# Weights before values: moving the second half of the up weights, its groups and the values' casts in a fused attention and feed-forward kernel

## The chip, the cores and the metric

The kernel runs on one core of a Trainium2 chip. The metric is the device time of one execution in microseconds (us). Six runs of the kernel before gave a median of 352.59 us (351.64 to 352.95).

The engines by their names in the profile: PE is TensorE (matmuls; PEld its weight loads), DVE is VectorE, ACT is ScalarE, POOL is GpSimd, SP is SyncE, which here only issues transfers. POOL computes and issues transfers, in one order.

## The reference

There are 8 sequences of 576 tokens, with 8 heads of 64 columns, and 16 beacon keys and values in front of each head's own. Attention is causal over the 576, and the beacons are seen by all. Its output, 4608 rows of 512 columns, goes through a two-layer feed-forward part with a leaky ReLU.

```
q, k, v: (8, 8, 576, 64); beacon_k, beacon_v: (8, 8, 16, 64)
k_all = concatenate([beacon_k, k], axis=2); v_all likewise
scores = q @ k_all^T / sqrt(64), causal over the 576, beacons always seen
a = softmax(scores);  attn = a @ v_all
x = attn as (4608, 512)
h = x @ w_in            # (512, 2048), the "up" weights
g = maximum(0.01 * h, h)
out = g @ w_out         # (2048, 512)
```

## The kernel before, in words

**Tiling.** Attention goes by head pairs. There are four pairs in a sequence, so g = 0 to 31; g = 0 to 3 is sequence 0, g = 4 to 7 is sequence 1. For each pair:

- `score(g, n)`, n = 0 to 3, makes a part of the transposed scores (L306) in one of two PSUM buffers, and ScalarE writes its exponential to `aT` (L315). There are four `aT` buffers.
- `masks(g)` zeroes the part above the diagonal, by four POOL instructions (L363).
- `value(g, half)` multiplies `aT` with the values and a column of ones (L394); VectorE takes the reciprocal of the sums (L403) and scales (L404) into `x_nat`. Half 0 has three row blocks and needs key blocks 0 to 2 of the values; half 1 has two and needs all five.
- `finish(g)` transposes `x_nat` on TensorE (L416), and VectorE copies it to `xT` (L421), the feed-forward input with d_model on the partitions. It also sets `ready`, the number of chunks of 512 tokens whose `xT` is whole: one after g = 3, two after g = 7.

The feed-forward part goes by these chunks (nine) and, in each, by groups of four matmuls. `moe1(i, fc)` computes 128 of the 2048 hidden columns of chunk i (L430, then ScalarE at L437); 16 groups make a chunk, and groups 0 to 7 need the first half of `w_in`, 8 to 15 the second. `moe2` does a quarter of one of four output blocks (L452); after four, VectorE copies the result (L461) and SP stores it. Quarters 0 and 1 use the first half of `w_out`, 2 and 3 the second.

**Order.** All five engines follow an order written out by hand: an instruction stands on its engine where the code has it. `fill()` puts one feed-forward group at its place: a first-layer group if `xT` is ready, a second-layer group if its chunk is through and enough first-layer groups are done, by turns when both can go. If neither can go it puts nothing.

**The values.** `load_v(b)` puts six fp32 transfers for a sequence on SP's queue (L213, L216, L218): the beacons, then the five key blocks (the first without its beacons). With `after` given, the first waits until another transfer has landed. `cast_v` turns key blocks to bf16 in `v_aug`, one instruction a block (L227), and needs the loads landed.

**Transfers on POOL's queue.** `load_w_in(half)` (L110) and `load_w_out(half)` (L114) load half of a weight matrix each, fp32 to bf16. `load_qk(b, grp, es)` loads q and k of two head pairs (grp 0 or 1) as bf16; `es` takes one of the two (L133). `load_beacon_k` (L175) loads the beacon keys of sequences 2 to 7.

**Transposing q and k.** In sequences 0 and 1, `t_q(g, which)` transposes on TensorE (L253) and copies on VectorE. From sequence 2 on, `permute` (POOL, L167) reorders, `turn_pairs` transposes by two transfers on SP (L271), and `in_order(g)` puts the result in order on POOL: the beacon columns (L284), then qT and kT (L286). The beacon columns come from `beacon_transposes` (TensorE L189, VectorE L194), which needs `cast_beacon_k`.

**Around the change.** The steps g = 5, 6, 7 and the beginning of g = 8 are written out one by one. Here sequence 1's scores, all of sequence 1's values and the 16 first-layer groups of chunk 0 share TensorE. From g = 8 on a loop spreads the groups evenly over eight slots a step.

Of the kernel before, what the change touches and what calls it, by code (L numbers as in the profile page):

```python
# [15 lines left out]
def kernel(  # L16
# [11 lines left out]
    nc = tc.nc  # L28
# [9 lines left out]
    NF = DF // 128  # L38
# [69 lines left out]
    def load_w_in(half):  # L108
        cols = slice(half * DF // 2, (half + 1) * DF // 2)
        return nc.gpsimd.dma_start(out=w_in_sb[:, :, cols], in_=w_in_r[:, :, cols])  # L110
# [98 lines left out]
    def load_v(b, after=None):  # L209

        t = rawpool.tile([128, NKB, H, D], FP32, name="v_raw")
        v_raws[b] = t
        first = nc.sync.dma_start(out=t[0:NB, 0], in_=beacon_v[b].rearrange("h p d -> p h d"))  # L213
        if after is not None:
            behind(first, after)
        nc.sync.dma_start(out=t[NB:128, 0], in_=v[b, :, 0:112].rearrange("h p d -> p h d"))  # L216
        for c in (1, 2, 3, 4):
            last = nc.sync.dma_start(  # L218
                out=t[0 : ROWS[c], c],
                in_=v[b, :, OFF[c] : OFF[c] + ROWS[c]].rearrange("h p d -> p h d"),  # L220
            )
        return last

    def cast_v(b, eng, c0=0, c1=NKB):
        t, dst = v_raws[b], v_bufs[b % 2]
        for c in range(c0, c1):
            eng.tensor_copy(out=dst[0 : ROWS[c], c, :, 0:D], in_=t[0 : ROWS[c], c])  # L227
# [240 lines left out]
    def fill():  # L468
        i1, fc = divmod(done1[0], NF)
        i2, n2 = divmod(done2[0], NF)  # L470
        can1 = i1 < ready[0] and (i1 < 2 or i2 > i1 - 2)
        can2 = i2 < NCH and i2 < i1 and done1[0] >= NF + 10
        if can1 and (turn[0] == 0 or not can2):
            moe1(i1, fc)
            done1[0] += 1
            turn[0] = 1
        elif can2:
            moe2(i2, n2 // 4, n2 % 4)
            done2[0] += 1
            turn[0] = 0  # L480
        return can1 or can2
# [24 lines left out]
    with order:  # L506
# [23 lines left out]
        def loads(g):  # L530
            b, hp = divmod(g, NPAIR)
            if g == 1:
                cast_v(0, nc.gpsimd, 0, 1)
                load_qk(1, 0, (0,))
                beacon_columns(3, nc.gpsimd)
                cast_v(0, nc.gpsimd, 1, 3)
                load_v(1, after=load_qk(1, 0, (1,)))
                load_w_in(0)
                cast_v(0, nc.gpsimd, 3, 5)
            elif g == 2:  # L540
                beacon_columns(4, nc.gpsimd)
            elif g == 3:
                load_qk(1, 1, (0,))
                beacon_columns(5, nc.gpsimd)
            elif g == 4:
                load_qk(1, 1, (1,))
                beacon_columns(6, nc.gpsimd)
            elif g == 5:
                beacon_columns(7, nc.gpsimd)
            elif g > 2 * NPAIR and b < B - 1 and hp > 1:  # L550
                turn_pairs(b + 1, hp - 2)
                if hp == 2:
                    load_v(b + 1)
# [27 lines left out]
        for g in range(NG + 3):  # L581
            if has(g):
                loads(g)

            if g < 5:

                score(g, 0)
                score(g, 1)
                t_q(g + 1, 0)
                t_q(g + 1, 1)  # L590
                if g == 1:
                    tri_in_psum()
                if g in (1, 2):
                    masks_by_tri(g - 1)
                if g == 4:
                    value(2, 0)
                if g < 2:
                    keep_busy(3)
                score(g, 2)
                if g < 2:  # L600
                    keep_busy(7)
                if g == 3:
                    value(0, 1)
                score(g, 3)
                if g < 2:
                    keep_busy(4)
                if g == 2:
                    value(0, 0)
                elif g == 3:
                    value(1, 0)  # L610
                    value(1, 1)
                    finish(0)
                elif g == 4:
                    value(2, 1)
                    finish(1)
                if g > 1:
                    masks(g)
                if g == 4:
                    value(3, 0)
                continue  # L620

            if g == 5:

                score(5, 0)
                value(3, 1)
                score(5, 1)
                finish(2)
                score(5, 2)
                finish(3)
                fill()  # L630
                score(5, 3)
                cast_v(1, nc.gpsimd, 0, 3)
                load_w_in(1)
                masks(5)
                fill()
                t_q(6, 0)
                t_q(6, 1)
                fill()
                fill()
                continue  # L640

            if g == 6:
                score(6, 0)
                score(6, 1)
                fill()
                t_q(7, 0)
                t_q(7, 1)
                fill()
                score(6, 2)
                score(6, 3)  # L650
                cast_v(1, nc.gpsimd, 3, 5)
                load_w_out(0)
                masks(6)
                load_w_out(1)
                load_beacon_k(2, B, nc.gpsimd)
                fill()
                fill()
                value(4, 0)
                value(4, 1)
                continue  # L660

            if g == 7:
                score(7, 0)
                score(7, 1)
                value(5, 0)
                finish(4)
                value(5, 1)
                score(7, 2)
                fill()
                score(7, 3)  # L670
                load_qk(2, 0)
                masks(7)
                value(6, 0)
                finish(5)
                fill()
                value(6, 1)
                fill()
                value(7, 0)
                finish(6)
                fill()  # L680
                value(7, 1)
                fill()
                fill()
                finish(7)
                continue

            if g == 8:
                load_qk(2, 1)
                cast_beacon_k(2, B, nc.gpsimd.tensor_copy)
                for grp in range(2):  # L690
                    for which in range(2):
                        permute(2, grp, which)
                    turn_pairs(2, grp)
                    if grp == 0:
                        load_v(2)
                while done1[0] + done2[0] < 22:
                    fill()
                beacon_transposes(2, B)
                while done1[0] + done2[0] < 32:
                    fill()  # L700
                in_order(8)
                in_order(9)


            chunks = chunks_with(g - 3) if g - 3 >= 2 * NPAIR else ready[0]
            groups = 2 * NF * chunks - done1[0] - done2[0]
            steps = NPAIR - (g - 2) % NPAIR if g > 2 * NPAIR + 5 else 2 * NPAIR + 6 - g
            n = -(-(groups - 1) // steps)
            slots = [0] * 8
            for i in range(n):  # L710
                slots[(2, 5, 1, 6, 0, 4, 3, 7)[i % 8]] += 1
            owed = [0]

            def slot(n):
                owed[0] += slots[n]
                while owed[0] and fill():
                    owed[0] -= 1

            if has(g):
                score(g, 0)  # L720
                score(g, 1)
            slot(0)
            if g - 3 >= 2 * NPAIR:
                finish(g - 3)
            slot(1)
            if g - 2 >= 2 * NPAIR and has(g - 2):
                value(g - 2, 0)
            slot(2)
            slot(3)
            if has(g):  # L730
                score(g, 2)
                score(g, 3)
                if has(g + 2):
                    in_order(g + 2)
            slot(4)
            if g - 2 >= 2 * NPAIR and has(g - 2):
                value(g - 2, 1)
            slot(5)
            slot(6)
            if has(g):  # L740
                masks(g)
                loads_after(g)
            slot(7)
            if g == 8:
                cast_v(2, nc.vector)
# [32 lines left out]
```

## Time and profile before

| what | value |
|---|---|
| median of 6 runs | 352.59 us |
| the profiled execution, its own time | 352.33 us |
| span of its profile | 350.5 us |
| TensorE busy | 339.6 us, 97% |
| POOL busy | 196.1 us, 56% |
| first-layer matmuls, L430 | 576, 139.4 us |
| second-layer matmuls, L452 | 592, 138.8 us |
| granted TensorE clock, mean | 0.999 |
| transfers of v_raw key blocks on SP, of 256 KB | 24, 4.9 us from issue to landing (median) |
| transfers of w_in halves on POOL, of 1024 KB | 2, 10.2 us (median) |

The span runs from the first to the last instruction in the profile; the execution's own time lies 1.83 us above it. Weights are given by the bytes that they take on the core, in bf16. A timeline line has its start and length in us and the instruction, with the engine's idle time before it and what ended that in brackets. Matmuls are pipelined, so the sum of their lengths is more than the time they take together. In the DMA view q0 is POOL's queue and q1 SP's; each line has packets, megabytes and the time of the packets as a share of 16 engines' time, which can pass 100% where packets overlap.

### The profile page before, as it was taken

The page shows a single profiled execution, that of the slowest core. Times are in us where ns is not written, and L with a number is a line of the kernel's source. Part 1 is how long each engine was busy: PE and PEld are TensorE (multiplying, and loading weights), DVE is VectorE, ACT ScalarE, POOL GpSimd, SP SyncE. Part 2 cuts the span into 40 slices and gives each one's busy share as a digit, 9 for nine tenths or more (in the row PEclk, how much of TensorE's full clock was granted, in tenths as well). Part 3 has the DMA queues.
Part 4 walks back from the last instruction along what each step waited for, and adds up shares of the span by engine and source line. Part 5 has one row for each costly group of instructions (what it writes and reads, how often), then busy time and mean ns, then how long its engine had stood idle before and what let it go on. Part 6 is the DMA issues. An engine that isn't in the chain of part 4 may idle for free.

```text
span 350.5 us, 7409 instructions
## 1 busy us (share of the span) xinstructions
PE 339.6 (97%) x3046; PEld 171.8 (49%) x3046; DVE 98.0 (28%) x242; ACT 187.3 (53%) x277; POOL 196.1 (56%) x335
## 2 busy tenths in 40 slices
PE   7999799999999999999999999999999999999996
PEld 6564454444554444445444444454444554444444
DVE  3793441023342123322322123222321331000121
ACT  4987746565456863487337833785358304633300
POOL 7592945779799799877886779667421100000000
PEclk9999999999999999999999999999999999999999
DMA  8999999968997794992489419980110011000012
GB/s 164 191 165 195 151 202 187 183 124 155 208 208 111 147 184 91 172 215 55 78 172 187 98 32 192 176 131 26 42 57 0 2 65 57 0 30 32 30 60 92
DMA packets 85121, 40.88 MB, mean 117 GB/s; under 512 B 69040, under 2 KB 79280, under 8 KB 85088
## 3 DMA queue, kind: packets, MB, share of 16 engines
q1 hardware_dynamic: 72544, 26.52, 36.5%
q0 software_dynamic: 12128, 13.54, 24.9%
q10 hardware_dynamic: 416, 0.36, 0.5%
q8 instruction: 24, 0.39, 0.5%
q14 instruction: 9, 0.07, 0.1%
HBM read 37.22 MB, written 9.44 MB: 133 GB/s over the span
## 4 chain that ended last, share of the span: by engine, by line
PE 85%; DMA 7%; ACT 4%; DVE 2%; SPq 0%; issue 0%; POOL 0%
PE acc L452 36%; PE acc L430 33%; PE av L394 7%; PE sc L306 7%; DMA v_raw<-in_v_dram 4%; ACT aT L315 3%; DMA w_in_sb<-in_moe_w_in_dram 3%; PE tp L416 2%; DMA v_raw<-in_k_dram 1%; DVE osb L461 1%; DVE xT L421 1%; SPq L216 0%; ACT k_nat L519 0%; SPq L218 0%; POOL v_aug L227 0%
## 5 line engine op out<-in xcount | busy, mean ns | idle before, releaser
L430 PE MATMUL acc<-xT,w_in_sb 128*128 128x512 bf16 x576 | 139.4, 379 | 4.2 <-DMA w_in_sb<-in_moe_w_in_dram 2.7
L452 PE MATMUL acc<-w_out_sb,gT 128*128 128x512 bf16 (+1 forms) x592 | 138.8, 374 | 0.0
L315 ACT ACTIVATE aT<-sc 128x1024 bf16<-128x1024 f32 (+3 forms) x128 | 103.8, 869 | 64.3 <-PE sc L306 60.4
L437 ACT ACTIVATE gT<-acc 128x512 bf16<-128x512 f32 x144 | 85.7, 601 | 77.6 <-PE acc L430 77.5
L430 PEld LDWEIGHTS <-w_in_sb 128*128 128x128 bf16 x576 | 51.7, 98 | 62.2 <-issue 4.6
L452 PEld LDWEIGHTS <-gT 128*128 128x128 bf16 x592 | 53.3, 98 | 58.6 <-issue 6.1
L461 DVE COPY osb<-acc 128x512 f32<-128x512 f32 (+1 forms) x37 | 25.1, 678 | 128.0 <-PE acc L452 126.9
L363 POOL TENSOR_SCALAR_AFFINE_SELECT aT<-aT 128x224 bf16<-128x224 bf16 (+1 forms) x120 | 48.6, 446 | 15.6 <-ACT aT L315 10.7
L286 POOL COPY qT<-q_turn 128x576 bf16<-128x576 bf16 x24 | 28.5, 1188 | 40.1 <-PE sc L306 21.2
L394 PEld LDWEIGHTS <-aT 128*128 128x128 bf16 (+1 forms) x960 | 36.7, 98 | 15.5 <-issue 2.2
L394 PE MATMUL av<-v_aug,aT 128*128 128x65 bf16 (+1 forms) x960 | 40.0, 194 | 0.3 <-issue 0.3
L306 PE MATMUL sc<-qT,kT 64*128 64x80 bf16 (+4 forms) x384 | 36.0, 283 | 1.6 <-ACT aT L315 1.1
L404 DVE TENSOR_TENSOR x_nat<-av,rec 128x384 bf16<-128x384 f32 x64 | 31.4, 491 | 2.2
L286 POOL COPY kT<-k_turn 128x576 bf16<-128x576 bf16 x24 | 28.5, 1186 | 0.8 <-DMA k_turn<-k_nat 0.6
L403 DVE RECIPROCAL rec<-av 128x6 f32<-128x6 f32 x64 | 11.9, 186 | 56.9 <-PE av L394 56.9
L227 POOL CAST v_aug<-v_raw 128x512 bf16<-128x512 f32 (+1 forms) x35 | 20.3, 623 | 12.1 <-DMA v_raw<-in_v_dram 12.1
L421 DVE COPY xT<-tp 128x576 bf16<-128x576 bf16 x32 | 14.5, 453 | 43.1 <-PE tp L416 43.1
L306 PEld LDWEIGHTS <-kT 64*128 64x128 bf16 x384 | 12.2, 94 | 27.3 <-issue 16.3
L133 POOL DMA_DIRECT2D q_raw<-in_q_dram x31 | 19.6, 631 | 4.7 <-DMA w_out_sb<-in_moe_w_out_dram 4.5
L133 POOL DMA_DIRECT2D k_raw<-in_k_dram x31 | 19.7, 634 | 2.7 <-PE acc L430 1.7
L167 POOL COPY q_nat<-q_raw 128x1152 bf16<-128x1152 bf16 x12 | 13.8, 1154 | 0.5 <-DMA q_raw<-in_q_dram 0.5
L416 PEld LDWEIGHTS <-x_nat 128*128 128x128 bf16 (+2 forms) x160 | 11.0, 97 | 6.3 <-DVE rec L403 0.2
(45 smaller groups left out, 93.0 us busy)
## 6 DMA issues: line engine op xcount, KB each, us to landing
out_dram<-osb SPq DMA_DIRECT2D x35, 256.0 KB, 2.3
v_raw<-in_v_dram SPq DMA_DIRECT2D x24, 256.0 KB, 4.9
q_raw<-in_q_dram POOLq DMA_DIRECT2D x31, 144.0 KB, 5.5
k_raw<-in_k_dram POOLq DMA_DIRECT2D x31, 144.0 KB, 5.8
w_in_sb<-in_moe_w_in_dram POOLq DMA_DIRECT2D x2, 1024.0 KB, 10.2
w_out_sb<-in_moe_w_out_dram POOLq DMA_DIRECT2D x2, 1024.0 KB, 12.4
v_raw<-in_v_dram SPq DMA_DIRECT2D x8, 224.0 KB, 3.5
v_raw<-in_v_dram SPq DMA_DIRECT2D x8, 160.0 KB, 4.7
```

The costliest lines, as they stand in the source:

```text
L133: dma = nc.gpsimd.dma_start(out=dst[e * RP : (e + 1) * RP], in_=src[b, h0 : h0 + 2].rearrange("h (p i) d -> p h i d", i=RI),)
L227: eng.tensor_copy(out=dst[0 : ROWS[c], c, :, 0:D], in_=t[0 : ROWS[c], c])
L286: nc.gpsimd.tensor_copy(out=dst.rearrange("c (p i) -> c p i", i=RI), in_=t[:, :, e].rearrange("c i p -> c p i"),)
L306: nc.tensor.matmul(out=sc[:, par, col - c0 : col - c0 + w], lhsT=kT[ps_, c * 128 : (c + 1) * 128], rhs=qT[ps_, q0 : q0 + w], start=True, s ...
L315: nc.scalar.activation(out=aT[:, :, c0 : c0 + w], in_=sc[:, :, 0:w], func=AF.Exp, scale=0.125)
L363: nc.gpsimd.affine_select(out=part, in_=part, compare_op=ALU.is_ge, fill=0.0, base=base, channel_multiplier=-1, pattern=pattern,)
L394: nc.tensor.matmul(out=avv[:, n, 0 : D + 1], lhsT=aT[0 : ROWS[c], par, a0 : a0 + 128], rhs=va[0 : ROWS[c], c, 2 * hp + par, :], start=(c = ...
L404: nc.vector.tensor_tensor(out=x_nat[:, t0:t1].rearrange("p t e d -> p (t e) d"), in0=avv[:, :, 0:D], in1=rec[:, n0:n1, None].to_broadcast( ...
L430: nc.tensor.matmul(out=acc, lhsT=w_in_sb[:, j, fc * 128 : (fc + 1) * 128], rhs=xT[:, j, i * 512 : (i + 1) * 512], start=(j == 0), stop=(j ...
L437: nc.scalar.activation(out=gT[i][:, fc, :], in_=acc, func=AF.Prelu, alpha=0.01)
L452: nc.tensor.matmul(out=acc[:, 0:w], lhsT=gT[i][:, fc, t * 128 : (t + 1) * 128], rhs=w_out_sb[:, fc, c0 : c0 + w], start=(fc == 0), stop=(f ...
L461: nc.vector.tensor_copy(out=osb[:, 0:w], in_=acc[:, 0:w])
```

## The change

- In g = 1, `load_v(1)` goes; it comes in g = 4, behind the last `load_qk(1, 1, (1,))`, and waits for that load. `load_w_in(1)` follows it at once; before, it stood in g = 5 behind the casts of values' key blocks 0 to 2.
- The casts of sequence 1's values move from g = 5 and 6 to g = 7, behind the scores of head pair 7. `load_w_out(0)` stands between them, and `masks(7)`, `load_beacon_k`, `load_qk(2, 0)`, `load_w_out(1)` and `load_qk(2, 1)` follow.
- `value(4, ...)` moves from the end of g = 6 to g = 7, behind `score(7, 3)` and four groups. In all, g = 7 has eight groups where it had six, so that the 16 groups of chunk 0 all stand ahead of `finish(7)`.
- In g = 8, `permute(2, 1)` and its `turn_pairs` move behind `in_order(8)` and `in_order(9)`, and these stand ahead of the loop that brings the count of groups to 32.
- The second layer may start when 28 first-layer groups are done; before, 26.

```diff
-        can2 = i2 < NCH and i2 < i1 and done1[0] >= NF + 10
+        can2 = i2 < NCH and i2 < i1 and done1[0] >= NF + 12
...
-                load_v(1, after=load_qk(1, 0, (1,)))
+                load_qk(1, 0, (1,))
                 load_w_in(0)
...
             elif g == 4:
-                load_qk(1, 1, (1,))
+                load_v(1, after=load_qk(1, 1, (1,)))
+                load_w_in(1)
                 beacon_columns(6, nc.gpsimd)
...
                 score(5, 3)
-                cast_v(1, nc.gpsimd, 0, 3)
-                load_w_in(1)
                 masks(5)
...
                 score(6, 3)
-                cast_v(1, nc.gpsimd, 3, 5)
-                load_w_out(0)
                 masks(6)
-                load_w_out(1)
-                load_beacon_k(2, B, nc.gpsimd)
-                fill()
-                fill()
-                value(4, 0)
-                value(4, 1)
+                fill()
+                fill()
                 continue
 
             if g == 7:
                 score(7, 0)
                 score(7, 1)
+                fill()
+                fill()
+                score(7, 2)
+                score(7, 3)
+                cast_v(1, nc.gpsimd, 0, 3)
+                load_w_out(0)
+                cast_v(1, nc.gpsimd, 3, 5)
+                masks(7)
+                load_beacon_k(2, B, nc.gpsimd)
+                load_qk(2, 0)
+                load_w_out(1)
+                load_qk(2, 1)
+                fill()
+                fill()
+                value(4, 0)
+                value(4, 1)
+                fill()
                 value(5, 0)
                 finish(4)
                 value(5, 1)
-                score(7, 2)
-                fill()
-                score(7, 3)
-                load_qk(2, 0)
-                masks(7)
+                fill()
                 value(6, 0)
                 finish(5)
-                fill()
                 value(6, 1)
                 fill()
                 value(7, 0)
                 finish(6)
-                fill()
                 value(7, 1)
-                fill()
                 fill()
                 finish(7)
                 continue
 
             if g == 8:
-                load_qk(2, 1)
                 cast_beacon_k(2, B, nc.gpsimd.tensor_copy)
-                for grp in range(2):
-                    for which in range(2):
-                        permute(2, grp, which)
-                    turn_pairs(2, grp)
-                    if grp == 0:
-                        load_v(2)
+                for which in range(2):
+                    permute(2, 0, which)
+                turn_pairs(2, 0)
+                load_v(2)
                 while done1[0] + done2[0] < 22:
                     fill()
                 beacon_transposes(2, B)
+                in_order(8)
+                in_order(9)
+                for which in range(2):
+                    permute(2, 1, which)
+                turn_pairs(2, 1)
                 while done1[0] + done2[0] < 32:
                     fill()
-                in_order(8)
-                in_order(9)
```

More of the change, by code (lines that the diff above doesn't have):

```diff
@@ L650 @@
                 score(6, 3)
+                masks(6)
+                fill()
+                fill()
+                continue
+            if g == 7:
+                score(7, 0)
+                score(7, 1)
+                fill()
[4 more added lines that the diff above has]
+                load_w_out(0)
                 cast_v(1, nc.gpsimd, 3, 5)
-                load_w_out(0)
-                masks(6)
+                masks(7)
+                load_beacon_k(2, B, nc.gpsimd)
+                load_qk(2, 0)
                 load_w_out(1)
-                load_beacon_k(2, B, nc.gpsimd)
+                load_qk(2, 1)
                 fill()
@@ L659 @@
                 value(4, 1)
[L660 to L664, printed above, removed]
+                fill()
                 value(5, 0)
```

## The prediction

> **What bounds the kernel now.** I read the page first: one execution, span 350.5 us, 352.33 us as timed (1.83 us lie around the span); the median of the six runs is 352.59. From the page: the busy times, and the slices of 8.8 us.
>
> ```profile
> PE 339.6 (97%) x3046; PEld 171.8 (49%) x3046; DVE 98.0 (28%) x242; ACT 187.3 (53%) x277; POOL 196.1 (56%) x335
> PE   7999799999999999999999999999999999999996
> POOL 7592945779799799877886779667421100000000
> DMA  8999999968997794992489419980110011000012
> ```
>
> TensorE sets the time: what it computes is the same before and after, so only its idle time, 10.9 us, can be won. The fifth digit, a 7, lies at 35 to 44 us, inside the stretch that is changed. The waits of TensorE after 28 us are two:
>
> ```profile
> PE acc L430 <- DMA w_in_sb<-in_moe_w_in_dram: 2.7, 1, 2.7
> PE acc L430 <- DVE xT L421: 1.4, 6, 0.2
> ```
>
> The windows view has no TensorE instruction between 41.26 and 43.94 us: 2.69 us of stall. The chain of waits (start, length, what) says why:
>
> ```profile
> 21.93 12.27 DMA v_raw<-in_v_dram
> ...
> 34.26 0.56 POOL v_aug L227
> 34.81 9.08 DMA w_in_sb<-in_moe_w_in_dram
> ...
> 43.94 1.04 PE acc L430 x4
> ```
>
> The second half of w_in is issued by POOL behind the casts of sequence 1's values, and these wait for their loads. POOL's timeline shows that wait, two later ones, and POOL's last step towards the scores of head pair 12 (columns: start, length, instruction, idle before it and its releaser):
>
> ```profile
> 32.67 1.17 POOL L227 CAST v_aug<-v_raw 128x512 bf16<-128x512 f32 x2 [6.27 <-DMA v_raw<-in_v_dram]
> 34.81 0.78 POOL L110 DMA_DIRECT2D w_in_sb<-in_moe_w_in_dram  x1
> 49.74 0.59 POOL L133 DMA_DIRECT2D k_raw<-in_k_dram  x1 [1.69 <-PE acc L430]
> 54.87 0.59 POOL L133 DMA_DIRECT2D q_raw<-in_q_dram  x1 [4.54 <-DMA w_out_sb<-in_moe_w_out_dram]
> 72.45 1.18 POOL L286 COPY qT<-q_turn 128x576 bf16<-128x576 bf16 x1 [3.15 <-DMA q_turn<-q_nat]
> 90.78 1.18 POOL L286 COPY kT<-k_turn 128x576 bf16<-128x576 bf16 x1
> ```
>
> From TensorE's timeline, the scores of pair 12, less than a microsecond after that copy ends:
>
> ```profile
> 92.88 0.58 PE L306 MATMUL sc<-qT,kT 64*128 64x512 bf16 x4
> ```
>
> Last, the DMA view by window gives rates (packets, MB, share). These lines are POOL's queue q0 in 22 to 24 and SP's queue q1 in 30 to 36, then q0 and q1 in 24 to 26, then q0 in 45 to 60:
>
> ```profile
> q0 software_dynamic: 145, 0.30, 100.2%
> q1 hardware_dynamic: 3611, 0.91, 79.7%
> q0 software_dynamic: 199, 0.32, 91.4%
> q1 hardware_dynamic: 188, 0.05, 16.9%
> q0 software_dynamic: 2789, 2.96, 116.7%
> ```
>
> So q0 alone moves 0.152 MB/us early (0.91 MB in 18 to 24) and 0.197 later; q1 alone 0.18 (0.91 MB, ended at 35.2); both together 0.178 in 20 to 30 (1.47 + 0.31 MB).
>
> **The change part by part.**
>
> *The stall removed.* load_w_in(1) is issued on POOL right behind load_qk(1, 1, (1,)), which ended at 24.3: at 24.3 instead of 34.81. It delays beacon_columns(6), masks(4) and beacon_columns(7) on POOL by its 0.8 us; POOL then idled 6.27 us, which hides it, and head pair 6's transposes read the first of them only at 30 us. TensorE is unchanged until 38.07 us, where value(4, 0) stood. Now score(7, 0) and (7, 1) come first (0.52, from 39.10 to 39.62), so the first group with second-half weights is due at 38.6. When do they land? At 24.0 q0 has 0.90 MB ahead of them (0.85 until 30, 0.05 after). Without values beside it that takes 4.7 us (at 0.193, the rate of both queues in 24 to 30) to 5.9 (at 0.152): 28.7 to 29.9. Then 1.05 MB: alone at 0.197 done at 34.0; at the 0.13 that q0 kept beside the values in 28 to 30, at 38.0; I take 36, between, because the values start a few us in (their first packets came 4.5 us after their first issue) and q0 then kept 0.16 (24 to 26). All three are ahead of 38.6: gain 2.69 us.
>
> Against this stands the Trainium skill, "DMA: Bandwidth & Descriptors", section Issuing engines are not separate DMA queues: transfers of all issuing engines share the same DMA engines and interleave. Read as equal bytes, w_in would run alone from 29.3 to 31.8, then at half of 0.193, and land at about 37.5, still in time; the rows give q0 six times q1's bytes in 24 to 26 and about twice in 28 to 30. The sum by that rule is the same within 0.1 us.
>
> *The values later.* SP's first load waits for k_raw of (1, 1), at 29 to 30 instead of 20.0. Nothing else is queued on SP until sequence 2's transposes at 55. Everything pending at 24 is 0.90 + 1.05 + 1.21 = 3.16 MB: at 0.193 done at 40.4; at 0.178 at 41.8; with 0.152 for q0 and 0.18 for the values behind it (5.9 + 6.9 + 6.7) at 43.5. I take 41.8, the same mix as 20 to 30. Key block 2 landed about 1.2 us ahead of the end before (34.1 against 35.2). POOL: masks(6) 37.9 to 39.5 (it was behind a 0.91 us issue), casts of blocks 0 to 2 to 41.3, load_w_out(0) 0.91, blocks 3 and 4 1.2: done at 43.4. TensorE is at value(4, 0) at 42.75 and needs block 4 at 43.4 (0.37 us into the second half's start, then 0.25): cost 0.1 us. At the 43.5 end, blocks 0 to 2 are cast at 42.95, block 4 at 45.05: cost 1.7. At the 40.4 end 0.
>
> *Groups and scores moved up.* Four groups and the four scores of head pair 7 now cover the values. score(7, 3) takes the buffer that the exp of (7, 1) frees: ACT ends its two evictions at 38.90 and two exps of 1.85 together at 40.75; TensorE comes at 40.5. Cost 0.25 (0 if one eviction is ahead, 0.5 with one more behind). Group evictions (0.55 each) follow within their four buffers; VectorE needs 1.8 us per head pair (rec to xT) against 2.2 us of TensorE's.
>
> *All 16 groups of chunk 0 before finish(7).* Before, two groups of chunk 0 stood behind finish(7) and hid its copy to xT (0.45). Now chunk 1's first group follows directly; three of its four matmuls don't need that copy. The row "acc <- DVE xT 1.4, 6" prices exactly that: 0.23 us. Cost 0.2.
>
> *Second-layer start from 26 to 28 groups.* Same matmuls, 0.864 us a group: 0. Its cover is w_out: half 0 issued at 41.3 lands by w_in's 9.1 at 50.4, and is due at 62; half 1 at 59.9 (5.3 behind the transfer before it, as from 49.2 to 54.5 before), due at 65.5. Beyond 5.6 us of lateness each further one would cost one.
>
> *POOL's order for sequence 2.* The issues move: w_out(0) 38.3 to 41.3, w_out(1) 40.7 to 48.2, beacon_k 41.6 to 45.0, load_qk(2, 0) 42.4 to 45.9, now ahead of w_out(1). Before, the second k_raw issue waited until w_out(0) had landed (49.74), the third q_raw until w_out(1) (54.87), the fourth k_raw until beacon_k (56.45): each waits for the eighth issue before it. Now those are w_out(0) at 50.4, beacon_k at 52.1 (1.7 behind, as before), q_raw at 52.6. POOL is through its issues at 53.3 instead of 57.04; q and k of (2, 0) land by 54.6. Cast 0.84, permute(2, 0) two of 1.1: 56.3; q_turn issued 55.3, usable 5.3 later, 60.6 (59.26 to 64.54 before). beacon_transposes after 22 groups at 56.9 waits for nothing. in_order(8) 60.6 to 62.9, in_order(9) to 65.2; score(8) is due at 65.9, 3.0 later. permute(2, 1) stands behind them now: q_turn issued at 66.3 instead of 68.03 (SP was held by load_v(2) until 67.94; it ends at 64.0 now), so in_order(10) and the POOL work chained to it through 92 us runs 1.7 us earlier. kT of pair 12 was ready at 91.96, 0.9 ahead of its score: the gain is capped at 0.9 + 1.7 = 2.6. Cost 0.
>
> **Sum:** 2.69 - 0.1 - 0.25 - 0.2 = 2.1 us, from the profiled 352.33 to 350.2; from the median, which is 0.26 above it, 350.5. I forecast 350.4. From 0.2% (0.7 us) on, a measurement of this kernel can tell a change from none.
>
> **The rivals.** (1) *The values' wait takes the weights' place, in part.* The 43.5 end above: 2.69 - 1.7 - 0.25 - 0.2 = 0.5; POOL's chain is then only 0.05 earlier, its cap 0.95. Time about 352.0. For it: q0 ran at 0.152 in 18 to 24. Against: 0.2 from 38 on.
>
> (2) *Slower: POOL held by late values.* Behind the casts on POOL stand masks(7), w_out, and all of sequence 2; what the values are late there, kT of pair 12 is late. If q_turn(2, 1) issues after 68.9 (0.9 behind today's 68.03, 2.6 behind my forecast; the values then end after 44.4), TensorE waits at score(12), whatever it won before. At the slowest stretch of the values alone (0.12 MB/us, mean of the slices of 32.0 to 32.5) 1.21 MB from 36.8 end at 46.9: 5.1 late, 2.5 over the point: 355.1. For it: no idle time on POOL in 89.6 to 117. Against: that rate lasted only half a microsecond.
>
> (3) *The weights still come late.* Slow q0 (29.9) and equal shares from 32.5: landing at 39.8 to 40.6, up to 2.0 stalled at the ninth group, the values then in time: gain 0.5, 352.1.
>
> (4) *All goes well:* no cost at 40.4 for values or scores: 2.5, 350.0; this is part of the forecast's case.
>
> **How the numbers follow.** Forecast with (4) 0.56; (1) 0.20, of it 0.12 a gain over 0.7; (2) 0.18; (3) 0.06, of it 0.04. Faster 0.56 + 0.12 + 0.04 = 0.72, same 0.10, slower 0.18. The forecast's own range is 349.5 to 351.3. To hold 8 in 10 it reaches from 349.4 (all 2.69 and the runs' 0.4 below their median) to 352.9, over (1) and (3), leaving out most of (2).
>
> **What would show it.** Right: no wait of acc on w_in near 41; w_in's landing between 34 and 38; last values' cast at 43 to 44; a new 0.2 us wait on xT at 51; score(8) near 66; no TensorE wait at score(12), near 90.8. Wrong: a TensorE wait of over 1 us on v_aug near 43, a wait on w_in at 38.6, or kT of pair 12 later than 91.96.

## The result, and the profile after

The changed kernel is slower: 354.17 us, the median of 36 runs, against 352.44 of 73 runs of the kernel before; the ratio is 1.0047 (95% interval 1.0034 to 1.0060), about 1.7 us. The profiled execution has a span of 351.9 us against 350.5. The forecast was 350.4, with a range of 349.4 to 352.9.

The page's busy times and slices of 8.8 us of the changed kernel:

```profile
PE 339.1 (96%) x3046; PEld 171.2 (49%) x3046; DVE 98.2 (28%) x242; ACT 186.9 (53%) x277; POOL 196.3 (56%) x335
PE   7999999799799999999999999999999999999996
POOL 7593664579799799977795779667421100000000
DMA  8999599969995792995389509990110011000012
```

TensorE's 7 at the fifth digit is gone, as forecast. Two new ones stand at the eighth digit (62 to 70 us) and the eleventh (88 to 97). POOL has idle time at the eighth too, where it had less before. The waits of TensorE (us in all, times, longest) name them:

```profile
PE sc L306 <- POOL kT L286: 4.1, 2, 2.3
...
PE acc L430 <- DVE xT L421: 1.4, 6, 0.2
...
PE acc L430 <- DMA w_in_sb<-in_moe_w_in_dram: 0.4, 1, 0.4
```

The 2.7 us wait for the second half of w_in is gone; the 0.4 that is left is the first half, at 27.9 us. In its place TensorE waits twice for kT, 4.1 us together. TensorE's timeline has the places, the scores of pair 8 and of pair 12:

```profile
67.55 0.58 PE L306 MATMUL sc<-qT,kT 64*128 64x512 bf16 x4 [2.33 <-POOL kT L286]
94.21 0.59 PE L306 MATMUL sc<-qT,kT 64*128 64x512 bf16 x4 [1.79 <-POOL kT L286]
```

Before, these scores stood at 68.07 and 92.88. So TensorE came to score(8) at 65.22, 2.85 us earlier than before; it lost 2.33 there and 1.79 at score(12), and from there it is 1.33 late, nearly to the end (the span is 1.4 longer). The chain of waits shows what was late at score(8):

```profile
51.01 5.09 PE acc L430 x24
56.09 8.94 DMA q_turn<-q_nat
...
66.34 1.15 POOL kT L286
...
67.55 0.58 PE sc L306 x4
...
93.01 1.15 POOL kT L286
```

The transpose of q for the first two pairs of sequence 2 takes 8.94 us from issue to landing; before, issued at 59.26, it took 5.2. The DMA view by window says what stood in the way. These are POOL's queue q0 and SP's queue q1 (packets, MB, share) of the changed kernel: q0 in 56 to 58, then both in 58 to 60, 60 to 62 and 62 to 64:

```profile
q0 software_dynamic: 411, 0.42, 124.7%
q0 software_dynamic: 369, 0.37, 110.7%
q1 hardware_dynamic: 151, 0.04, 11.2%
q1 hardware_dynamic: 453, 0.12, 148.2%
q0 software_dynamic: 89, 0.09, 25.8%
q1 hardware_dynamic: 349, 0.09, 86.9%
q0 software_dynamic: 16, 0.01, 6.9%
```

The transpose is issued at 56.09, but SP's queue moves nothing until 58, and hardly anything until most of what POOL's queue holds (w_out's second half, then q and k of (2, 1)) is through at about 61. From 61 to 64 POOL's queue moves only 0.04 MB more (its last k_raw lands at 64.21), and yet SP's moves only 0.13: for about 3 of the 8.94 us little moves at all, and no run here shows why. Before, the transpose was issued when POOL's queue was nearly empty. The same view of the kernel before, q0 in 58 to 60, then both in 60 to 62:

```profile
q0 software_dynamic: 279, 0.28, 84.6%
q1 hardware_dynamic: 1149, 0.29, 76.7%
q0 software_dynamic: 25, 0.02, 7.0%
```

POOL's and SP's timelines of the changed kernel carry the delay on to pair 12 (start, length, instruction, idle before it and its releaser):

```profile
65.15 1.15 POOL L286 COPY qT<-q_turn 128x576 bf16<-128x576 bf16 x1 [7.55 <-DMA q_turn<-q_nat]
69.78 1.17 POOL L167 COPY q_nat<-q_raw 128x1152 bf16<-128x1152 bf16 x1
74.41 1.17 POOL L286 COPY qT<-q_turn 128x576 bf16<-128x576 bf16 x1 [2.04 <-PE sc L306]
```

```profile
63.33 0.74 SPq L213 DMA_DIRECT2D v_raw<-in_beacon_v_dram  x1
64.58 3.77 SPq L218 DMA_DIRECT2D v_raw<-in_v_dram  x4
70.98 1.28 SPq L271 DMA_TRANSPOSE q_turn<-q_nat  x1
```

POOL sits idle for 7.55 us inside in_order(8), and permute(2, 1), which the change put behind in_order(9), runs only at 69.78. Its transpose goes out at 70.98 instead of 68.03, and the copy for pair 10 starts at 74.41 instead of 72.45. The releaser named in that row, the scores, was done long before; the transpose landed 3.3 us after its issue, at 74.3. From there POOL's chain runs about 2 us late to kT of pair 12, done at 94.16 instead of 91.96.

### The profile page after: what moved, and what is told of

Its sections match the earlier page's. It is cut to its first block, busy times and chain, and to the rows that moved or that the text cites. A ratio compares the mean times of both kernels' runs of the same rounds, so it can differ in the third digit from the quotient of the medians.

```text
span 351.9 us, 7407 instructions
## 1 busy us (share of the span) xinstructions
PE 339.1 (96%) x3046; PEld 171.2 (49%) x3046; DVE 98.2 (28%) x242; ACT 186.9 (53%) x277; POOL 196.3 (56%) x335
## 4 chain that ended last, share of the span: by engine, by line
PE 85%; DMA 9%; DVE 2%; POOL 2%; issue 0%; SPq 0%; ACT 0%; POOLq 0%
PE acc L452 35%; PE acc L430 33%; PE av L394 7%; PE sc L306 7%; DMA w_in_sb<-in_moe_w_in_dram 3%; DMA q_turn<-q_nat 3%; DMA v_raw<-in_v_dram 2%; PE tp L416 2%; DMA v_raw<-in_k_dram 1%; DVE osb L461 1%; DVE xT L421 1%; POOL qT L286 1%; POOL kT L286 1%; PE tp L253 0%; POOL v_aug L227 0%
## 5 line engine op out<-in xcount | busy, mean ns | idle before, releaser
L167 POOL COPY k_nat<-k_raw 128x1152 bf16<-128x1152 bf16 x12 | 13.9, 1160 | 0.0
```

## The experiments

Theory T: transposes by transfer, on SP's queue, get next to nothing while POOL's queue is full; POOL's order passes the delay on. Each ratio is against runs of the kernel before that were taken along with the variant (their medians lie between 352.26 and 353.05), so it is not the time over 352.44.

Some profiles have a stretch with TensorE's granted clock at half: about 3.4 us between 68 and 74 us in e2_permute_first, e3_start_26 and e8_wout1_behind (0.91 on the mean of 60 to 80), as much between 43 and 47 in e7_before_loads, about 7 us from 19 on in e4_first_part. A run's mean clock tells of it: it is 0.998 or more, or mostly 0.994 to 0.995. The kernel before has medians of 351.80 to 352.02 us over its runs at 0.998 or more, and was 1.1 to 2.1 us slower at 0.994 to 0.995. That is as much as the change costs, so where it matters, runs at 0.998 or more are compared below; there the changed kernel has 353.56 (352.74 to 354.60). A profile with such a stretch doesn't show how long TensorE would have waited behind it.

**Without the transfer that stands in front.**

```diff
+        nc.vector.memset(w_out_sb[:, NF // 2 :, :], 0.0)
...
                 load_qk(2, 0)
-                load_w_out(1)
                 load_qk(2, 1)
```

> The changed kernel without the transfer of w_out's second half; VectorE fills that half with zeros at the start, so the result is not the reference's. Theory T (sequence 2's transposes by transfer stand behind POOL's queue, which w_out's second half keeps full until about 61 us): q_turn of (2, 0) is usable about 5 us after its issue instead of 8.9; no TensorE wait at score(8); the wait at score(12) shrinks from 1.8 to at most 1.2; the span falls from 351.9 to about 349, the time to about 0.992 of the changed kernel's, under the kernel before. Rival R (a pair of transposes issued so close together needs 9 us by itself, or POOL's order alone is at fault): q_turn still needs 8 to 9 us and the 2.3 us wait at score(8) stays; time as the changed kernel's, 1.005 of before.

Measured: 349.96 us, ratio 0.9916 (0.9886 to 0.9946), span 347.6. The transpose was issued at 54.89 and landed 3.9 us later. POOL's timeline:

```profile
58.90 1.18 POOL L286 COPY qT<-q_turn 128x576 bf16<-128x576 bf16 x1 [1.35 <-DMA q_turn<-q_nat]
```

TensorE waits for kT neither at score(8) nor at score(12); the second wait was to shrink to 1.2 and went altogether, if narrowly (kT of pair 12 is done 0.05 us before its scores start, at 89.91). So neither wait comes without the transfer in front, and without them the first part of the change gives somewhat more than was forecast for it (span 2.9 below before, forecast 2.1). This kernel also moves 1 MB less, which could help elsewhere.

**The order of g = 8 put back.**

```diff
                 turn_pairs(2, 0)
                 load_v(2)
+                for which in range(2):
+                    permute(2, 1, which)
+                turn_pairs(2, 1)
                 while done1[0] + done2[0] < 22:
                     fill()
                 beacon_transposes(2, B)
                 in_order(8)
                 in_order(9)
-                for which in range(2):
-                    permute(2, 1, which)
-                turn_pairs(2, 1)
```

> The changed kernel with only the order of g = 8 put back: permute(2, 1) and its turn_pairs ahead of in_order(8) and in_order(9). Theory T: the 2.3 us wait at score(8) stays (q_turn lands as late as before), but POOL does permute(2, 1) in its idle 57.6 to 65.2, so q_turn(2, 1) is issued at about 68.4 instead of 70.98, in_order(10) and kT of pair 12 come 1.6 to 2 us earlier, and the 1.8 us wait at score(12) nearly goes: time 1.5 to 1.8 below the changed kernel's, level with before (ratio 1.000). Rival P (order of POOL alone is the whole loss): both waits go, ratio 0.99. Rival N (order of POOL has no part): nothing changes, ratio 1.005.

Measured: 353.43 us, ratio 1.0006 (0.9971 to 1.0040). The waits for kT are one, at score(8):

```profile
67.93 0.59 PE L306 MATMUL sc<-qT,kT 64*128 64x512 bf16 x4 [1.90 <-POOL kT L286]
```

The wait at score(8) stays and the one at score(12) is gone, as theory T has it; but this profile doesn't show that POOL's order did it. These are POOL's copy of kT and the scores of pair 12 here, then the same scores in e3_start_26, the next run, which keeps the change's order:

```profile
92.83 1.17 POOL L286 COPY kT<-k_turn 128x576 bf16<-128x576 bf16 x1
94.42 0.58 PE L306 MATMUL sc<-qT,kT 64*128 64x512 bf16 x4
94.66 0.59 PE L306 MATMUL sc<-qT,kT 64*128 64x512 bf16 x4
```

kT of pair 12 is done at 94.00, only 0.16 us earlier than in the changed kernel, where 1.6 to 2 was expected. TensorE takes 26.5 us from score(8) to score(12) where it took 24.8 before, with the stretch at half clock among them; and e3_start_26, with that stretch too, has next to no wait there (0.09) without the new order. The times at a clock of 0.998 or more tell it better: 351.36 to 352.65 us here (four runs), all below the changed kernel's 352.74 to 354.60, and level with the kernel before. So POOL's order has a part of about 1.6 us there, as theory T expected. Over all runs the ratios (1.0006 and 1.0047) say the same in their middles and not in their intervals.

**The second layer from 26 groups on, as before.**

```diff
-        can2 = i2 < NCH and i2 < i1 and done1[0] >= NF + 12
+        can2 = i2 < NCH and i2 < i1 and done1[0] >= NF + 10
```

> The changed kernel with the second layer's start put back from 28 to 26 groups. Theory T: no part in the loss, ratio as the changed kernel's, 1.005 within 0.002. Rival: the later start leaves a first-layer group in the way or an eviction on ScalarE; then 0.5 us or more is gained.

Measured: 354.43 us, ratio 1.0033 (1.0003 to 1.0063): not told apart from the changed kernel. The wait at score(8) is 2.5 us. At a clock of 0.998 or more the median is 353.44 us (four runs), against 353.56. This edit has no visible part.

**The first part alone.** The early weights, casts, groups and values of g = 5 to 7 as in the change; the rest as before.

```diff
-                load_beacon_k(2, B, nc.gpsimd)
-                load_qk(2, 0)
                 load_w_out(1)
+                load_beacon_k(2, B, nc.gpsimd)
+                load_qk(2, 0)
                 load_qk(2, 1)
```

(with the two edits of the runs above)

> Only the first part of the change: the weights' second half ahead of the values, the casts, groups and values of g = 5 to 7 as in the change; the order of sequence 2's loads (w_out's second half ahead of the beacons and q and k), of g = 8 and the start at 26 groups as before. Theory T: the stall on w_in is gone and score(8) is due near 65; POOL's queue drains at about 61 to 62 as ever, so q and k of (2, 0) land at 59, q_turn lands near 65 and TensorE waits 1 to 2 us at score(8); score(12) waits 0.5 to 1: time 0 to 1 us under before. Rival (the loss comes from the new order of sequence 2's loads and of g = 8): no waits at score(8) and score(12), time 2.5 to 3 us under before, ratio 0.992.

Measured: 354.02 us, ratio 1.0021 (0.9991 to 1.0052): no gain. Neither theory had the wait that came, and the one that theory T expected at score(8) is not there; TensorE's timeline:

```profile
61.48 0.51 PE L189 MATMUL tp<-ident,bk 128*128 128x128 bf16 x6 [2.87 <-POOL bk L180]
```

In that order the beacon keys stand behind both halves of w_out, and their transposes come 2.87 us late. The stretch at half clock hardly makes this wait: it has put both sides late by about the same, POOL by 2.4 us (its casts start at 41.42 instead of 39.05) and TensorE by 2.5 (it is due at these transposes at 58.61, in the changed kernel at 56.08). So the new order of sequence 2's loads was not superfluous: by these profiles, each of the two orders gives back what the first part won, at another place.

**The first wait covered, and nothing else.**

```diff
-                while done1[0] + done2[0] < 32:
+                while done1[0] + done2[0] < 35:
```

> The changed kernel with 35 groups instead of 32 ahead of score(8) and nothing else. Theory T: the wait at score(8) is covered, but kT of pair 12 still comes at 94 us by POOL's chain, so that TensorE waits longer at score(12), 2 to 4 us instead of 1.8, and nothing is gained: ratio 1.003 to 1.006. Rival S (each wait is a loss of its own): 2.3 us gained, ratio 0.998.

Measured: 354.02 us, ratio 1.0047 (1.0025 to 1.0070), as the changed kernel. TensorE's timeline, pairs 11 and 12:

```profile
85.45 0.59 PE L306 MATMUL sc<-qT,kT 64*128 64x512 bf16 x4 [0.94 <-POOL kT L286]
93.99 0.58 PE L306 MATMUL sc<-qT,kT 64*128 64x512 bf16 x4 [1.82 <-POOL kT L286]
```

There is no wait at score(8), and 0.94, 1.82, 0.25 and 0.84 us at pairs 11 to 14, in sum nearly the 4.1 us of the changed kernel. They did not all come at score(12), as was expected. The two waits were one loss: POOL's chain sets the time up to there, and a wait on it that is covered comes back later.

**The new order of loads in the kernel before.**

```diff
                 score(7, 3)
                 load_qk(2, 0)
+                load_w_out(1)
                 masks(7)
...
-                load_w_out(1)
                 load_beacon_k(2, B, nc.gpsimd)
```

> The kernel before with only the order of sequence 2's loads as in the change (w_out's second half behind load_qk(2, 0)). Theory T (transposes stand behind POOL's queue): q and k of (2, 0) land some 5 us earlier and q_turn is issued near 55 instead of 59.3, but it is usable only at 62 to 64.5, 8 to 9 us after its issue; time as before, ratio 0.999 to 1.002. Rival R (a transfer's transpose needs 4 to 5 us whenever issued): q_turn usable at 60.

Measured: 352.78 us, ratio 1.0005 (0.9976 to 1.0034). q_turn was issued at 54.83 and landed after 8.1 us, k_turn after 8.4: issued 4.4 us earlier than before, q_turn was there about 1.5 us earlier. Theory T holds with the rest of the change left out.

**The weights behind the transposes.**

```diff
                 load_qk(2, 0)
-                load_w_out(1)
                 load_qk(2, 1)
...
                     permute(2, 0, which)
+                load_w_out(1)
                 turn_pairs(2, 0)
```

> The changed kernel with w_out's second half issued by POOL only behind permute(2, 0), at about 57 us, so that only q and k of (2, 1) stand in front of the transposes. Theory T: q_turn is usable 4 to 6 us after its issue, by 61; no wait at score(8); w_out's second half lands at 65 to 68, due at 65.5, so up to 2.5 us of TensorE wait there; score(12) waits 0 to 1: ratio 0.992 to 0.999. Rival: the transposes, already begun, are slowed by the weights that come 2 us behind them, 8 us or more: ratio 1.003 or above.

Measured: 356.80 us, ratio 1.0123 (1.0089 to 1.0158). The rival named here was right. The transfer of the weights, issued at 55.96, took most of the DMA engines' time from transposes issued at 54.95 and 56.84: q_turn needed 6.8 us, k_turn 12.4, and the weights themselves 12.7. TensorE's timeline, and both queues in 60 to 62:

```profile
70.50 0.99 PE L306 MATMUL sc<-qT,kT 64*128 64x512 bf16 x4 [5.32 <-POOL kT L286]
```

```profile
q0 software_dynamic: 156, 0.16, 79.5%
q1 hardware_dynamic: 117, 0.03, 13.6%
```

Theory T has to be wider: a transpose suffers from what POOL's queue carries while it runs, not only from what stood there before it. The two together moved 0.10 MB/us here, half of what q0 moved alone in 56 to 58 us of the changed kernel (0.42 MB).

**w_out's first half ahead of the casts.**

```diff
-                cast_v(1, nc.gpsimd, 0, 3)
                 load_w_out(0)
-                cast_v(1, nc.gpsimd, 3, 5)
+                cast_v(1, nc.gpsimd)
```

> The changed kernel with load_w_out(0) ahead of the casts of sequence 1's values (39.0 instead of 40.7 us), nothing else. Theory T (what counts is when POOL's queue has drained): it drains 1 to 1.7 us earlier, q_turn of (2, 0) is usable 1 to 1.7 us earlier, near 63.5, and the waits at score(8) and score(12) shrink by that much in sum: ratio 0.999 to 1.002. Rival: the last key blocks of the values, or value(4, 1), become late beside the weights, and nothing is gained: ratio 1.004 or more.

Measured: 353.10 us, ratio 1.0016 (0.9993 to 1.0038). POOL's copy of qT for pair 8 starts at 63.69, 1.46 earlier than in the changed kernel, and the two waits are 1.00 and 1.76, 1.4 less in sum: as expected. The transpose itself took longer (10.2 us), for it was issued 2.7 us earlier; what counts is when POOL's queue is through. The time shows less of it than the profile: at a clock of 0.998 or more the median is 353.10, 0.5 us under the changed kernel's.

**A better version.** First the transposes of (2, 1) ahead of the values, with 35 groups.

```diff
                 turn_pairs(2, 0)
+                for which in range(2):
+                    permute(2, 1, which)
+                turn_pairs(2, 1)
                 load_v(2)
...
                 in_order(9)
-                for which in range(2):
-                    permute(2, 1, which)
-                turn_pairs(2, 1)
-                while done1[0] + done2[0] < 32:
+                while done1[0] + done2[0] < 35:
```

> The changed kernel with permute(2, 1) and its turn_pairs ahead of load_v(2) and of in_order(8), and 35 groups instead of 32 ahead of score(8). Theory T: the transposes of both groups still wait for POOL's queue to drain near 61 to 62, but (2, 1)'s follow at once, not behind the values: q_turn(2, 1) issued at 63 to 66, kT of pairs 8, 9 and 10 ready by 67.5, 70 and 72; score(8), due at 67.6, waits 0 to 0.5 and score(12) not at all: time 0.990 of before (about 4 us under the changed kernel). Rival: the values, loaded behind the transposes, come late on VectorE and hold back the output copies or value(8): ratio above 0.996.

Measured: 351.15 us, ratio 0.9954 (0.9931 to 0.9977), faster than before, but half of what was expected: TensorE still waits for kT, 0.60 at score(8) and 0.25 and 0.84 at pairs 13 and 14. This kernel differs from e6_groups_35 in the place of permute(2, 1) and its turn_pairs alone, and both are set against the same runs of the kernel before: 0.9954 against 1.0047, 2.9 us by their medians (2.7 at a clock of 0.998 or more). So that place has a large part in the loss, beside the transfer in front. None of its 12 runs has the stretch at half clock; against runs of the kernel before at the same clock (351.80) the gain is 0.65 us. Then the edit of e9 was added:

> The changed kernel with permute(2, 1) and its turn_pairs ahead of load_v(2) and in_order(8), 35 groups ahead of score(8), and load_w_out(0) ahead of the casts. Theory T: POOL's chain is 1 to 1.7 us earlier than with the first two alone, and the 1.7 us that TensorE waited there for kT at score(8), (13) and (14) nearly go: ratio 0.990 to 0.993. Rival: the waits return elsewhere (values on VectorE), ratio 0.995 as without it.

Measured: 350.83 us, ratio 0.9954 (0.9930 to 0.9979): nothing more. The expectation failed. POOL's timeline shows that its chain hung on something else there:

```profile
71.80 1.17 POOL L286 COPY qT<-q_turn 128x576 bf16<-128x576 bf16 x1 [2.29 <-issue]
```

The copy for pair 10 starts just after the scores of pair 8 end (71.20 to 71.7), whose qT buffer it takes; 35 groups ahead of score(8) had put these scores off. A third buffer tells. It leaves 5.66 KB a partition for the output buffers, which need 6, so the room for the beacon keys is cut as well (not in these lines):

```diff
+    qpool = ctx.enter_context(tc.tile_pool(name="qpool", bufs=3))
...
-        qT = headpool.tile([128, S], BF16, name="qT")
+        qT = qpool.tile([128, S], BF16, name="qT")
```

> The kernel e10_both with three buffers for qT instead of two (bk_raw's room is cut from 8 to 6 sequences to make place). Theory Q: in e10_both POOL's copy of qT for pair 10 waited 2.29 us, until 71.8, for the scores of pair 8, whose buffer it takes; that wait, not the transposes, held POOL's chain and left TensorE 1.0 us of waits at score(13) and (14). With a third buffer the copy starts near 69.5, the two waits go, and the time is 0.5 to 1.2 us lower: ratio 0.991 to 0.994. Rival: the transposes of (2, 1) or POOL's own work hold it: copy still at 71 to 72, ratio 0.995.

Measured: 350.39 us, ratio 0.9932 (0.9909 to 0.9955), span 348.3. The same copy, one source line further down, follows at once:

```profile
70.70 0.20 POOL L285 COPY kT<-bkT 128x16 bf16<-128x16 bf16 x1
70.84 1.16 POOL L287 COPY qT<-q_turn 128x576 bf16<-128x576 bf16 x1
```

It came 1.0 us earlier, not 2.3, because permute(2, 1) could start at 63.78 in this profile and at 61.35 in the other (it waits for q_raw); from that copy to the one for pair 14 POOL takes 30.5 us in both. The waits at pairs 13 and 14 are gone and one of 0.28 at score(8) is left. The buffer explains the waits; that the step from 0.9954 is real, the intervals alone don't show. This version is the fastest that computes the reference, 0.7% under the kernel before, or 0.5% (350.39 against 352.02 us) where only runs at a clock of 0.998 or more are compared.

## Why the prediction was wrong

**Right.** The stall and its removal: w_in's second half landed at 36.2 us (24.42 and 11.8; forecast 36), the values' last cast ended at 42.8 (forecast 43.4), and no wait for values or weights is left near 43. The costs on the way (0.1, 0.25 and 0.2) were over-estimated: none shows as a wait of TensorE between 28 and 65 us, the 0.2 on xT at 51 neither, and TensorE was due at score(8) at 65.2, not 65.9. POOL's issues moved as worked out: the last one ended at 54.15 (53.3), q_turn was issued at 56.09 (55.3).

**The step that failed** is the next one in "POOL's order for sequence 2": q_turn "usable 5.3 later, 60.6 (59.26 to 64.54 before)". It was usable at 65.03, 8.94 after its issue. The 5.3 was a duration from a moment when POOL's queue had run nearly dry. The change moved the transpose to a moment when, by the prediction's own landing time of 59.9 for w_out's second half, with q and k of (2, 1) still behind it, that queue was full. Both numbers stood in the text; the duration was moved without the traffic around it. With 8.94 in place of 5.3, kT of pair 8 would have come at 66.5 by the same sum, behind the 65.9 at which it was due. (It came at 67.49, with the issue 0.8 later.)

**The cost of zero for permute(2, 1)** behind in_order(9) fell with it: its transpose was put at 66.3 and came at 70.98, and POOL's chain was not 1.7 us earlier but 2.2 later (kT of pair 12 done at 94.16 against 91.96, the prediction's own sign of being wrong). Of the 2.2 us, 0.7 stand at kT of pair 8 already (67.49 against 66.82); the other 1.5 come behind it, where permute(2, 1) had to wait for in_order(9). Less the 0.9 of slack that kT of pair 12 had before, that is the 1.3 us by which TensorE is late.

**Rival (2)** had the place and the point right: with q_turn(2, 1) later than 68.9, TensorE waits at score(12). Its cause, late values, was wrong, and with it its price of 355.1: the values were in time, the transposes late. Rivals (1) and (3) did not come.

**The rule of the Trainium skill** weighed in the prediction (DMA: Bandwidth & Descriptors, Issuing engines are not separate DMA queues: transfers of all issuing engines share the same DMA engines and interleave) was applied to the weights against the values, where it cost nothing. It had to be applied to the transposes: there 0.37 MB against 0.04 in 58 to 60 us show that they share, and far from equally.

## What to carry to other kernels

A transfer's duration belongs to the traffic around it (3.9 to 10.5 us here for one and the same transpose): when a change moves an issue, read the queues at the new time, not at the old one. Where another engine's chain runs just ahead of TensorE for many steps (kT of pairs 12 to 14 was ready 0.9 to 1.4 us ahead of its scores before the change), a gain on TensorE is worth only what that chain can follow, and a wait that is covered by other work comes back at the chain's next step. Free buffers count in that chain too. And a stretch at a lower clock can hide a wait that an edit did not remove: compare runs at the same clock.

## What the runs showed of the hardware

- Transposes by transfer on SP's queue, beside a full queue of POOL's: 8.1 to 10.5 us from issue to landing for q_turn in the nine profiles in which w_out's second half stood in front of it; 3.9 where that was left out (e1_no_wout1) and 4.8 where q_turn was issued only at 62.5 (e4_first_part). In the nine, q_turn landed 0.5 to 2.3 us after the last k_raw on POOL's queue, whenever it had been issued. With the weights issued between the two transposes, 12.4 for k_turn.
- Transposes beside POOL's transfers can leave both slower than either alone: 0.10 MB/us together in 60 to 62 us of e8_wout1_behind and 0.06 in 61 to 64 of the changed kernel, against 0.2 for POOL's queue alone in 56 to 58 us there and 0.16 for SP's alone in 58 to 60 of e1_no_wout1.
- A run of one core can hold a stretch at half the granted clock with the rest at 1.0. In the profiles of e2, e3, e7 and e8 it lasts about 3.4 us and begins within 1.4 us of the end of a TensorE wait of 1.9 to 5.3 us; the kernel before and the changed kernel have waits of 2.7 and 2.3 us in their profiles without it, and in e4_first_part it comes at 19 us behind a wait of 0.5. The four kernels with no TensorE wait above 0.9 us after the first 10 us (e1, e5, e10, e12) have a mean clock under 0.998 in 1 of 41 runs, the kernel before in 44 of the 96 taken along with the variants, and e8, with its wait of 5.3 us, in all 6. That the waits bring it about is likely by these counts and not shown.
